# Retention plus gated MLP on one core: loads held behind TensorE products, and a new order of all engines' work

## The chip, the core and the metric

The kernel runs on one core of a Trainium2 chip. The metric is the device time of one execution in microseconds, the median over several runs. A profiled execution gives a trace of every engine; its span goes from the first to the last instruction, and a little lies around it.

## The reference

Inputs are q, k, v of shape 4 x 8 x 768 x 64 (batch, heads, tokens, head size) and the weights of a gated layer of width 512. First a retention layer runs over the tokens:

```
state = gamma[h] * state + outer(k[t], v[t])
y[t]  = q[t] @ state / sqrt(64)
```

Its heads side by side are x (4 x 768 x 512). Then:

```
gate = sigmoid(sum over 5 taps of conv_w[i] * x[t - 4 + i])
out  = (gate * (x @ w_val)) @ w_out
```

## The kernel before, in words

**Tiles.** Tokens are cut into 6 chunks of 128. One tile of q, k, v and k again by token, for one batch and one chunk, is "att" number g (0 to 23, four batches for each chunk); it is 1 MB, or 768 KB in chunk 0, where the fourth part is made on chip. Four att buffers rotate (LB = 4).

**Attention.** The four tiles of chunk 0 have steps of their own: turn (L338, a transpose), wide_scores (L251), wide_mask (L289, VectorE), wide_y (L307) and wide_state (L326). For every later g, TensorE runs block(g) (function block): outputs from the masked scores (y_scores, L348), the state update of this tile and of the next one (L228), outputs from the state (y_state, L348) and the scores of tile g + 1 (L207). Before it VectorE has to mask the scores (mask, L216), ScalarE has to copy the state (snap, L238), and GpSimd has to weigh the values of tile g + 1 by the decay (decay, L198). VectorE then takes the result out of PSUM (evac, L401).

**Weights.** The eight weight tiles (512 KB each) come as 64-bit floats and are converted by some five VectorE steps with help from ScalarE and GpSimd (cv_bits L466 and L472, cv_top L478, cv_exp L484, cv_rest L488, cv_round L512, cv_low L516) into a high and a low part.

**Gated layer.** For each chunk n and each quarter m of the width: four convolution taps on VectorE (tap, L529) and one on ScalarE (L527), a sigmoid (L536), twelve TensorE products val(n, m, 0 to 11) (L543), the gating product on VectorE (gated, L552), a rounded and a rest part (L559 ScalarE, L563 GpSimd). Then, for each batch b, twelve products outp(n, b, 0 to 11) (L571), a copy (store, L581) and the DMA out (send, L585). A val or outp product is one 128x128 by 128x512 matmul; there are 576 of them (some of the last ones cut in halves). Two PSUM buffers ("mm") hold their sums, so a third tile waits until the first has been taken out.

**What sets the order.** The code first collects 1,217 steps (function `at`), each with its engine and what it reads and writes, sorted by a due time. The tuple TURNS then lists the numbers of these steps in the order in which they are issued; `plan` only asserts that the list is allowed. Every engine and every DMA queue executes its own steps in the order of TURNS, and waits in place when the next one isn't ready. All loads and stores go through SyncE's queue (SP), apart from the small fall table. A load waits only until its buffer is free. A -1 in TURNS is a fill: one 128x512 matmul on zeros (function fill, L313), which computes nothing. There are 17.

Of the kernel before, what the change touches and what calls it, by code (L numbers as in the profile page):

```python
# [16 lines left out]
P = 128  # L17
# [8 lines left out]
GV = 6  # L26
TINY = 2.0 ** -15 * (1.0 + 1.0 / 8.0 - 2.0 ** -23)
# [20 lines left out]
def plan(steps, turns, fill):  # L48

    steps = sorted(steps, key=lambda s: s.due)  # L50
# [36 lines left out]
    return [steps[i] if i >= 0 else fill for i in turns]  # L87
# [3 lines left out]
def tile_retention_gated_mlp(  # L91
# [32 lines left out]
    nc = tc.nc  # L124
# [37 lines left out]
    steps = []  # L162
# [11 lines left out]

    def load(g, part=slice(0, 4)):
        b, c = chunks[g]
        i = b * NCH + c
        if g not in tiles:
            tiles[g] = loads.tile([P, 4, 2, 2, P], F32, name="att")
        src = att[i, :, part]  # L180
        if g in PIECES_OF:
            size = P * 4 * P
            src = att[i].rearrange("p a x j n -> (p a x j n)")[part.start * size:part.stop * size].rearrange(
                "(p a x j n) -> p a x j n", p=P, x=2, j=2, n=P
            )
        nc.sync.dma_start(out=tiles[g][:, part], in_=src)  # L186
# [125 lines left out]
    def fill():  # L312
        nc.tensor.matmul(  # L313
            z_ps[:, 0].rearrange("p b j e -> p (b j e)"),
            lhsT=warm.broadcast_to([P, P]), rhs=warm.broadcast_to([P, 512]),
            start=not begun, stop=True, skip_group_check=True,
        )
# [103 lines left out]
    def load_w(n):  # L421
# [7 lines left out]
        nc.sync.dma_start(out=st, in_=src)  # L429
# [108 lines left out]
    def val(n, m, i):  # L538
# [4 lines left out]
        nc.tensor.matmul(  # L543
# [4 lines left out]
        )  # L548
# [16 lines left out]
    def outp(n, b, i, cs):  # L565
        if i == 0:
# [4 lines left out]
        nc.tensor.matmul(  # L571
            ops[n, b, cs.start][:, 0:cs.stop - cs.start],
            lhsT=gg[:, b * P:(b + 1) * P],
            rhs=w[:, ct, cs],
            start=(i == 0), stop=(i == 3 * NPAIR - 1),
        )
# [11 lines left out]
    def first_sigmoid():  # L588
# [345 lines left out]
    with tc.manual_schedule():  # L934
        for step in plan(steps, TURNS, Step(0.0, "PE", 0.2345, [], [], fill, ())):
            step.fn(*step.args)
# [104 lines left out]
```

## Time and profile before

| | |
|---|---|
| median of 3 runs | 212.74 us (212.64 to 212.78) |
| profiled execution | 212.19 us, span 210.5 us |
| TensorE busy in the span | 200.7 us (95%) |
| VectorE, ScalarE, GpSimd busy | 135.7, 110.1, 105.6 us |
| DMA | 35.18 MB, mean 167 GB/s |

The busy times are means over stages that differ: until about 47 us the engines share the start, afterwards TensorE works without a gap that matters. So the table says little about the start, which has to be read by stretches, by the chain of work that ended last, and by timelines of single engines.

### The profile page before, as it was taken

How to read it: one execution, taken by the hardware profiler on the slowest of the kernel's cores; microseconds unless marked ns; L12 is line 12 of the kernel's file. 1: busy time of each engine (PE TensorE's matmuls, PEld its weight loads, DVE VectorE, ACT ScalarE, POOL GpSimd, SP SyncE). 2: the span in 40 equal slices, each digit the busy share in tenths (PEclk: the TensorE clock that was granted, in tenths of full speed). 3: DMA queues.
4: the chain of work that ended last, by engine and by line, in shares of the span. 5: the costliest groups of instructions: out<-in, count | busy, mean ns of one | idle time of the engine just before them, and what ended most of it. 6: DMA issues, size and time to landing. Idle time of an engine off the chain costs nothing.

```text
span 210.5 us, 7499 instructions
## 1 busy us (share of the span) xinstructions
PE 200.7 (95%) x3322; PEld 159.9 (76%) x3325; DVE 135.7 (64%) x209; ACT 110.1 (52%) x228; POOL 105.6 (50%) x98
## 2 busy tenths in 40 slices
PE   8699699999899999999999999999999999999993
PEld 3578477778678888888888878787878777877783
DVE  1987999999999952469528791625867357671000
ACT  2478988598736925382534643516460654523321
POOL 1477699899964238830266731422920456132200
PEclk9999889999999999999999999999999999999998
DMA  6999998576602984519725270011110111111122
GB/s 214 375 417 379 402 404 307 198 291 218 223 14 69 360 350 178 206 52 348 277 79 156 101 246 23 35 55 53 53 50 0 50 53 50 50 50 50 51 102 100
DMA packets 8402, 35.18 MB, mean 167 GB/s; under 512 B 937, under 2 KB 1193, under 8 KB 5810
## 3 DMA queue, kind: packets, MB, share of 16 engines
q1 hardware_dynamic: 8352, 34.66, 44.5%
q8 instruction: 26, 0.43, 0.9%
q10 hardware_dynamic: 18, 0.04, 0.1%
q14 instruction: 6, 0.05, 0.1%
HBM read 28.41 MB, written 6.29 MB: 165 GB/s over the span
## 4 chain that ended last, share of the span: by engine, by line
PE 79%; DVE 9%; DMA 4%; ACT 2%; issue 2%; SPq 1%; DVEq 0%; ACTq 0%
PE mm L571 32%; PE mm L543 28%; PE sy L348 9%; DMA att<-in_att_dram 4%; DVE acc L529 3%; PE sy L207 3%; PE z_ps L228 3%; PE z_ps L326 1%; PE sy L251 1%; DVE top L478 1%; SPq L186 1%; DVE acc L484 1%; PE mm L307 1%; DVE acc L472 1%; DVE rest L488 1%
## 5 line engine op out<-in xcount | busy, mean ns | idle before, releaser
L529 DVE SCALAR_TENSOR_TENSOR acc<-x,cw_sb,acc 128x512 f32<-128x512 f32 x96 | 69.4, 751 | 7.2 <-ACT acc L527 6.4
L563 POOL TENSOR_TENSOR gvl<-gate,gvh 128x512 fp32r<-128x512 f32 x24 | 31.0, 1293 | 51.9 <-ACT gvh L559 50.8
L581 ACT COPY o_sb<-mm 128x512 f32<-128x512 f32 (+1 forms) x25 | 14.2, 569 | 47.2 <-PE mm L571 47.1
L571 PE MATMUL mm<-woh,gvh 128*128 128x512 f32 (+1 forms) x100 | 38.9, 393 | 0.0
L571 PE MATMUL mm<-wol,gvh 128*128 128x512 f32 (+1 forms) x100 | 38.5, 387 | 0.0
L571 PE MATMUL mm<-woh,gvl 128*128 128x512 f32 (+1 forms) x100 | 38.4, 386 | 0.0
L552 DVE TENSOR_TENSOR gate<-mm,gate 128x512 f32<-128x512 f32 x24 | 16.6, 690 | 33.0 <-PE mm L543 30.4
L414 POOL TENSOR_TENSOR xl<-x,xh 128x512 fp32r<-128x512 f32 x24 | 30.6, 1289 | 11.0 <-ACT xh L410 11.0
L543 PE MATMUL mm<-xh,wvh 128*128 128x512 f32 x96 | 32.3, 413 | 1.3 <-ACT xh L410 1.3
L198 POOL TENSOR_TENSOR att<-att,first_sb 128x512 f32<-128x512 f32 x24 | 25.0, 1047 | 15.7 <-DMA att<-in_att_dram 13.0
L543 PE MATMUL mm<-xh,wvl 128*128 128x512 f32 x96 | 30.4, 399 | 0.7 <-issue 0.7
L543 PE MATMUL mm<-xl,wvh 128*128 128x512 f32 x96 | 30.3, 397 | 0.5 <-POOL xl L414 0.5
L536 ACT ACTIVATE gate<-acc 128x512 f32<-128x512 f32 x24 | 14.4, 598 | 16.9 <-DVE acc L529 11.1
L571 PEld LDWEIGHTS mm<-woh,gvh 128*128 128x128 f32 x100 | 18.7, 188 | 5.4 <-ACT o_sb L581 1.3
L543 PEld LDWEIGHTS mm<-xh,wvl 128*128 128x128 f32 x96 | 18.0, 188 | 5.5 <-issue 1.0
L543 PEld LDWEIGHTS mm<-xh,wvh 128*128 128x128 f32 x96 | 17.4, 188 | 6.0 <-ACT xh L410 1.4
L571 PEld LDWEIGHTS mm<-woh,gvl 128*128 128x128 f32 x100 | 18.8, 188 | 4.1
L543 PEld LDWEIGHTS mm<-xl,wvh 128*128 128x128 f32 x96 | 17.8, 188 | 5.1 <-POOL xl L414 1.2
L571 PEld LDWEIGHTS mm<-wol,gvh 128*128 128x128 f32 x100 | 18.8, 188 | 3.7
L401 DVE TENSOR_TENSOR x<-sy,dec 128x512 f32<-128x512 f32 x20 | 13.8, 688 | 10.2 <-PE sy L207 9.4
L559 ACT CAST gvh<-gate 128x512 fp32r<-128x512 f32 x24 | 14.9, 619 | 6.9 <-DVE gate L552 4.4
L410 ACT CAST xh<-x 128x512 fp32r<-128x512 f32 x24 | 14.6, 622 | 6.2 <-DVE x L401 3.1
(65 smaller groups left out, 266.1 us busy)
## 6 DMA issues: line engine op xcount, KB each, us to landing
att<-in_att_dram SPq DMA_DIRECT2D x20, 1024.0 KB, 6.1
out_dram<-o_sb SPq DMA_DIRECT2D x23, 256.0 KB, 2.1
wst<-in_w_dram SPq DMA_DIRECT2D x7, 512.0 KB, 7.7
att<-in_att_dram SPq DMA_DIRECT2D x3, 768.0 KB, 8.3
first_sb<-in_first_dram SPq DMA_DIRECT2D x1, 568.0 KB, 3.9
att<-in_att_dram SPq DMA_DIRECT2D x1, 512.0 KB, 5.0
att<-in_att_dram SPq DMA_DIRECT2D x1, 256.0 KB, 6.0
out_dram<-o_sb SPq DMA_DIRECT2D x2, 128.0 KB, 1.8
```

What stands on the lines that cost most here:

```text
L198: nc.gpsimd.tensor_tensor(v, v, vd_sb[:, c, :].unsqueeze(2).broadcast_to([P, 8, HALF]), op=ALU.mult)
L348: return nc.tensor.matmul(sy[cols, h, off:off + HALF], lhsT=lhsT, rhs=rhs, start=start, stop=True, skip_group_check=True,)
L410: nc.scalar.copy(xh[n, ct], xs[n][:, ct, :, HALO:])
L414: nc.gpsimd.tensor_tensor(xl[n, ct], xs[n][:, ct, :, HALO:], xh[n, ct].bitcast(F32), op=ALU.subtract)
L529: nc.vector.scalar_tensor_tensor(acc, x[:, :, k:k + P], cw_sb[:, m, k:k + 1], acc, op0=ALU.mult, op1=ALU.add,)
L536: nc.scalar.activation(gate[n, m], accs.pop((n, m)), AF.Sigmoid)
L543: nc.tensor.matmul(vps[n, m], lhsT=w[:, m, ct * P:(ct + 1) * P], rhs=xx[n, ct].rearrange("p b t -> p (b t)"), start=(i == 0), stop=(i == 3 ...
L552: nc.vector.tensor_tensor(gv, vps.pop((n, m)), gv, op=ALU.mult)
L559: nc.scalar.copy(gvs[n, m][0], gate[n, m])
L563: nc.gpsimd.tensor_tensor(gvl, gate.pop((n, m)), gvh.bitcast(F32), op=ALU.subtract)
L571: nc.tensor.matmul(ops[n, b, cs.start][:, 0:cs.stop - cs.start], lhsT=gg[:, b * P:(b + 1) * P], rhs=w[:, ct, cs], start=(i == 0), stop=(i ...
L581: nc.scalar.copy(o_sb[:, 0:step], ops.pop((n, b, cs.start))[:, 0:step])
```

## The change

It has three parts.

**Loads held.** Every val and outp product is appended to a list. Each load (att tiles and weight tiles, not the stores) that is issued when at least four products are in the list gets one more wait: on the fourth-last product issued so far. With the new order that holds for 19 loads: att 8 to 23 and weight tiles 5, 4 and 7.

**Fills of two sizes.** A -1 is a fill of 512 columns, a -2 one of 128. The new list has five -1 and four -2. The six fills with which TensorE began are gone; it begins with one fill of 128, first_pos and the two outer steps.

**A new TURNS.** The same 1,217 steps in another order, on all engines and queues. From block(22) on TensorE's order is the old one. Before, among other things:

- loads begin: weight 0, att 0 (q and k), weight 1, att 1, att 3, att 0 (v), att 2, weights 3 and 2, att 4, 5, 6, weight 6, att 7, 8, 9, weights 5 and 4. Before: weight 0, att 0 (q, k), att 0 (v), weight 2, att 1, att 2, weight 3, att 3, weight 1, att 4, 5, weight 4, att 6, weight 6, att 7, weight 7, att 8, weight 5;
- the table counts what lies ahead of some blocks in either list:

| ahead of | VectorE steps up to its mask, before / after | products, before / after |
|---|---|---|
| block(4) | 30 / 30 | 1 / 2 |
| block(6) | 48 / 48 | 24 / 24 |
| block(8) | 65 / 62 | 42 / 44 |
| block(9) | 70 / 70 | 48 / 52 |
| block(10) | 79 / 77 | 69 / 69 |
| block(12) | 94 / 95 | 85 / 89 |
| block(13) | 100 / 99 | 108 / 120 |
| block(15) | not counted | 139 / 168 |
| block(17) | not counted | 163 / 240 |

- tiles of the gated layer come in another order (in chunk 0 the stores go out as b = 3, 1, 0, 2);
- stores and loads are mixed differently on SP. Att 22 is now the last load: it stands behind outp(2, 0, 7), so it waits for outp(2, 0, 4). Of its tile, block(21) needs the decayed values. TensorE's list between the two is: outp(2,0) 5 to 9, val(3,2) 9 to 11, block(20), outp(2,1) 0 to 8, five more outp, block(21).

The diff, with TURNS cut:

```diff
@@ -24,6 +24,7 @@
 GV = 6
+LAG = 4
-def plan(steps, turns, fill):
+def plan(steps, turns, fills):
...
-    return [steps[i] if i >= 0 else fill for i in turns]
+    return [steps[i] if i >= 0 else fills[-1 - i] for i in turns]
...
+    products = []
+
+    def hold(dma):
+
+        if len(products) >= LAG:
+            tc.add_manual_dep(
+                dma.ins, products[-LAG].ins.name,
+                mybir.DependencyInfo(mybir.DependencyClass.Sync, mybir.DependencyReason.DATA),
+                reason="loads keep clear of the fetch of the program",
+            )
+
     def load(g, part=slice(0, 4)):
...
-        nc.sync.dma_start(out=tiles[g][:, part], in_=src)
+        hold(nc.sync.dma_start(out=tiles[g][:, part], in_=src))
...
-    def fill():
+    def fill(size):
         nc.tensor.matmul(
-            z_ps[:, 0].rearrange("p b j e -> p (b j e)"),
-            lhsT=warm.broadcast_to([P, P]), rhs=warm.broadcast_to([P, 512]),
+            z_ps[:, 0].rearrange("p b j e -> p (b j e)")[:, 0:size],
+            lhsT=warm.broadcast_to([P, P]), rhs=warm.broadcast_to([P, size]),
...
-        nc.sync.dma_start(out=st, in_=src)
+        hold(nc.sync.dma_start(out=st, in_=src))
...
-        nc.tensor.matmul(
+        products.append(nc.tensor.matmul(
             vps[n, m],
...
-        nc.tensor.matmul(
+        products.append(nc.tensor.matmul(
             ops[n, b, cs.start][:, 0:cs.stop - cs.start],
...
     TURNS = (
-        12, -1, 6, 4, 5, 0, 13, 11, -1, 1, 14, -1, 16, -1, 15, -1, 19, -1, 18, 8, 17, 7, 10, -1, 20, -1, 28,
+        12, 6, 5, 1, 2, 13, 11, 4, 0, 20, 15, 17, 14, 19, -2, 28, 8, 29, 7, 18, 10, 46, 59, 60, 21, 53,
+        16, 70, 22, -2, -1, -2, -1, -1, 32, 81, 61, 62, 63, 64, 23, 65, 24, 66, 33, 9, 26, 25, 94, 35,
...
     with tc.manual_schedule():
-        for step in plan(steps, TURNS, Step(0.0, "PE", 0.2345, [], [], fill, ())):
+        for step in plan(steps, TURNS, [Step(0.0, "PE", 0.2345, [], [], fill, (n,)) for n in (512, 128)]):
             step.fn(*step.args)
```

## Rows read from the trace of the kernel before

**Rows 1.** The page: span, and busy us (share) with count by engine.
```profile
span 210.5 us, 7499 instructions
PE 200.7 (95%) x3322; PEld 159.9 (76%) x3325; DVE 135.7 (64%) x209; ACT 110.1 (52%) x228; POOL 105.6 (50%) x98
```

**Rows 2.** Stretches: length, busy us (instructions) by engine, granted TensorE clock, DMA share, GB/s.
```profile
20.00:25.00 5.00, 3.12 (x82) 2.31 (x83) 4.57 (x8) 4.79 (x11) 3.37 (x5) 0.97 1.02 407
25.00:30.00 5.00, 4.87 (x133) 4.24 (x134) 4.91 (x8) 4.02 (x9) 3.90 (x4) 0.69 1.00 408
45.00:50.00 5.00, 4.92 (x141) 4.00 (x140) 5.00 (x9) 5.00 (x14) 5.00 (x5) 1.00 0.63 220
150.00:155.00 5.00, 5.00 (x23) 3.82 (x21) 4.12 (x7) 1.31 (x3) 2.76 (x3) 1.00 0.15 56
```

**Rows 3.** The chain that ended last: start us, us, what.
```profile
24.93 0.76 DVE acc L529
...
46.45 0.61 DVE u L216
...
47.11 0.69 PE sy L348 x32
...
49.20 1.60 PE mm L543 x6
50.81 0.69 PE sy L348 x32
...
54.78 0.71 issue
...
67.18 0.62 PE sy L348 x32
...
103.76 1.64 PE mm L571 x7
...
125.41 0.62 PE sy L348 x32
...
127.28 0.67 PE mm L543 x2
...
194.00 12.78 PE mm L571 x65
```

**Rows 4.** VectorE between the masks of blocks 4 and 9: timeline, then the stretch.
```profile
23.39 0.68 DVE L216 TENSOR_TENSOR u<-sy,tri_sb 128x512 f32<-128x512 f32 x1
...
49.47 0.69 DVE L216 TENSOR_TENSOR u<-sy,tri_sb 128x512 f32<-128x512 f32 x1
...
23.39:49.47 26.08, 25.41 (x41) 0.93 0.78 297
```

**Rows 5.** TensorE's timeline at the start: start us, us, line, what, count [idle before <-releaser].
```profile
0.84 2.72 PE L313 MATMUL z_ps<-const-float32-0.0 128*128 128x512 bf16 x6 [0.84 <-PEq L1028]
...
10.94 1.16 PE L251 MATMUL sy<-att 64*128 64x128 f32 x16 [0.25 <-DMA att<-in_att_dram]
12.03 0.66 PE L338 MATMUL mm<-eye_sb,att 128*128 128x128 f32 x4
12.95 0.63 PE L338 MATMUL mm<-eye_sb,att 128*128 128x128 f32 x4 [0.26 <-DMA att<-in_att_dram]
...
20.42 1.05 PE L307 MATMUL mm<-gvl,att 128*64 128x128 f32 x16
21.85 0.46 PE L228 MATMUL z_ps<-att 64*64 64x64 f32 x16 [0.39 <-POOL att L198]
22.14 0.65 PE L207 MATMUL sy<-att 64*64 64x64 f32 x32
...
25.12 1.14 PE L348 MATMUL sy<-u,att 64*64 64x64 f32 x32 [0.31 <-issue]
...
28.75 1.34 PE L543 MATMUL mm<-xh,wvh 128*128 128x512 f32 x4
```

**Rows 6.** Att loads: SP's waits for TensorE, landing times; the decay step on GpSimd.
```profile
SPq L186 <- PE sy L348: 36.9, 11, 7.3
...
DMA to landing us min/median/max: 4.8/6.1/9.6
...
L198 POOL TENSOR_TENSOR att<-att,first_sb x24: 1042/1046/1056, 9.6 to 126.9; 128x512 f32<-128x512 f32 x24
```

More of the change, by code (lines that the diff above doesn't have):

```diff
@@ L547, in val @@
             start=(i == 0), stop=(i == 3 * NPAIR - 1),
-        )
+        ))
     def gated(n, m):
@@ L575, in outp @@
             start=(i == 0), stop=(i == 3 * NPAIR - 1),
-        )
+        ))
     def store(n, b, cs=slice(0, DM)):
```

127 rows, old and new, of the table TURNS are left out of this document.

## The prediction

> **What bounds the kernel now.** First the page: TensorE is busy 95% of the span [rows 1], so the question is where its other time lies. The stretches answer that: from 45 us on TensorE fills nearly every stretch, at a granted clock of 1.00; between 20 and 30 us it is busy for 3.12 of 5 us, and then works at a mean granted clock of 0.69, while VectorE is busy 4.57 to 5.00 of 5 us throughout [rows 2]. The chain names the bound of each part: from 24.93 us it runs nearly without a break over VectorE, up to the mask of block(8) at 46.45; from 47.11 to 206.78 us it is TensorE's own work, apart from one gap of 0.71 us at 54.78 in which TensorE waits for nothing that the profile shows [rows 3]. So whatever is gained has to come out of the first 50 us or out of that gap; the TensorE work from 67.18 to 206.78 us [rows 3] is fixed, since the change moves steps and removes none but fills.
>
> **Before VectorE's chain: the mask of block(4).** The old list reached this mask at 23.39 us, when VectorE came to it; the scores that it reads had been written at about 22.79 (22.14 and 0.65) [rows 4, 5]. Both lists put 30 VectorE steps up to it. What changes is the loads. In the old queue 568 + 512 + 256 + 512 + 768 + 768 = 3384 KB were queued up to att 2, and TensorE got it at 12.95; 768 KB earlier att 1 at 10.94 [rows 5], so 768 KB take 2.0 us. In the new queue the values of att 0 end at the same 3384 KB, so about 12.95 us, and att 2 768 KB later, so 14.96, 0.2 us before it is asked for. By 12.95 TensorE has done the first two score tiles and three transposes. From 12.95 on the old list needed until about 21.33 (20.42 and some 0.9) for two transposes, two score tiles, four state steps and three wide_y [rows 5]; that is 8.38 us. The new list has one wide_y more (1.02) and one transpose fewer (0.6) to do: 8.8 us, so 21.75. The old one then went on at 21.85 after 0.39 us of waiting for GpSimd, and its scores came 0.94 us later; the new one gives 22.7. I take 22.7 for the mask of block(4): 0.7 us earlier. Bounds: 22.2 if a load comes half a microsecond earlier, 24.4 if the clock is half (below).
>
> **VectorE from block(4) to block(12).** Between the masks of blocks 4 and 9 VectorE ran 40 steps in 26.08 us and was busy for 25.41 of them [rows 4], so 0.652 us a step with all its waits. In the new list the same two masks are 40 steps apart too, but four more products stand ahead of block(9) (52 against 48). VectorE therefore stays the bound for longer, down to block(12), where 95 steps stand ahead against 94, with 89 products against 85. The mask of block(12) then starts 95 - 30 = 65 steps behind that of block(4), 65 x 0.652 = 42.4 us, at 65.1; block(12) follows 0.66 us after its mask starts (46.45 to 47.11 [rows 3]): 65.75. TensorE by itself would not be later: block(9) at 22.7 + 26.08 + 0.66 = 49.4, then three blocks of 2.09 (47.11 to 49.20) and 0.2 for the slower product behind each (0.67 for two at 127.28 where two others take 0.47), and 37 products of 0.233 (1.64 for seven) [rows 3] give 64.9. That leaves 0.85 us for a gap such as the one at 54.78, which is gone or hidden here.
>
> **The sum.** The old block(12) started at 67.18 us [rows 3]. The new one starts 1.43 us earlier, and 4 products (0.93 us) fewer are left behind it. Behind block(12) VectorE is no bound: the mask of block(13) is four steps further (2.6 us), while TensorE has 31 products and a block ahead (9.5 us). So TensorE ends 2.36 us earlier. The profiled execution took 212.19 us; less 2.36 that is 209.83. The median of the runs shown lies 0.55 above it, so I predict 210.4 us.
>
> **What I cost at nothing.** Twelve 512-column fills fewer and four small ones more: the old ones ran while TensorE waited for loads or VectorE, so that their time becomes waiting. The held loads: most already waited for the block that frees their buffer (SP stood 36.9 us in 11 waits for TensorE [rows 6]), and their fourth-last product lies ahead of that block or within a dozen products behind it, ten microseconds or more ahead of the block that needs the tile. Att 20 and 22 are held longer; only att 22 is close, see (d). Behind a held load SP queues stores, whose four buffers reach four tiles back. GpSimd's decay of att 8 now stands ahead of that of att 7, which block(6) needs: att 8 is released some 4 us behind the start of block(4) and landed in 6.1 us at the median [rows 6], so both decays (1.05 us each) end near the moment when block(6) asks for them; VectorE's next step that reads block(6) comes seven steps later and covers a microsecond.
>
> **Half clock.** TensorE began with six fills, 2.72 us long [rows 5]. At 25.12 us, after the thin stretch, block(4) took 3.63 us (to 28.75) where block(8) took 2.09 [rows 2, 3, 5]. Those six fills go. [...] If only the first score tile runs at half speed, its 1.1 us more end before att 1 lands, about 10.3 us, and cost nothing: my sum. If the run behind 12.95 us is slow for as long as block(4) was, 1.7 us are lost in it.
>
> **Rivals.** (a) *Half clock in the run of chunk 0*: the mask of block(4) at 24.4, the gain 0.66 us, 212.1. For it: fewer fills, and TensorE still waits for loads. Against it: the fills that stay, and transposes that are drawn forward into the wait. (b) *VectorE denser*: 0.61 us a step, as between 25 and 30 us (8 steps, 4.91 us busy [rows 2]); then TensorE's own 64.9 shrinks with block(9) to 63.2 and decides, and the gain is 67.18 - 63.2 + 0.93 = 4.9 at most, 207.9; a gap of 0.71 makes it 208.6. (c) *The change doesn't do what it says*: the held loads don't change what TensorE waits for, steps on VectorE take 0.69 us because conversions wait for ScalarE and GpSimd in line, and 65 x 0.038 = 2.5 us are given back: 212.9. (d) *Slower: att 22 comes late.* It waits for outp(2,0,4). Between that and the state update in block(21) lie 22 products (5.13 us), block(20) (127.28 - 125.41 = 1.87, and 0.2) and 0.62 us of block(21): 7.8 us [rows 3]. In them the load must be issued (0.3), land and be decayed (1.05): it may take 6.4 us. Landings took 4.8 to 9.6 us, 6.1 at the median [rows 6]. TensorE has no slack there, so each microsecond beyond is lost in full: at 9.6 us 3.2 are lost, 213.6, slower than before by 0.8. It is slower than before from 8.8 us on. Against it: the long landings belong to the start, when 400 GB/s were moved [rows 2]; at 150 us the DMA engines are 15% busy.
>
> **How the numbers follow.** My forecast has a chance of 0.54, (a) 0.12, (b) 0.10, (c) 0.08, (d) 0.16. A measurement tells 0.2%, 0.43 us, from no change. The forecast and (b) are faster by more, and half of (a): 0.70. Half of (a) and half of (c) are the same: 0.10. The other half of (c) and (d) are slower: 0.20. The range takes in (b) with its gap, (a), (c) and most of (d): 208.6 to 213.2. The forecast's own range is 209.2 to 211.8, by 0.2 us on the mask of block(4) and 0.02 us on a step either way.
>
> **What would show it.** Right: the chain goes over VectorE until about 65 us and then over TensorE alone; the mask of block(4) starts near 22.7, that of block(9) near 48.8, and block(12) near 65.8; no gap at TensorE behind that. Wrong: a clock of 0.5 behind 12 us; the chain leaving VectorE at block(8) as before; GpSimd waiting for a load ahead of a decay and TensorE for that decay, above all before block(21); gaps at TensorE in which it waits for nothing that shows, each of them a loss once TensorE is the bound.

## The result and the profile after

The changed kernel took **210.12 us** (median of 4 runs, 209.52 to 211.15), the kernel before 212.76 (212.64 to 213.04) beside it: a ratio of 0.9884, with a 95% interval of 0.9853 to 0.9915. Run again beside the experiments it gave 0.9916 (0.9883 to 0.9948). The profiled execution took 210.03 us, against the 209.83 of the sum. Its page, to set beside [rows 1]; the last line is the share of the chain that ended last:

```profile
span 208.3 us, 7483 instructions
PE 199.1 (96%) x3317; PEld 160.4 (77%) x3317; DVE 136.2 (65%) x209; ACT 110.3 (53%) x228; POOL 105.8 (51%) x98
...
PE 82%; DMA 7%; POOL 4%; ACT 3%; issue 1%; DVE 0%; ACTq 0%; POOLq 0%; SPq 0%
```

VectorE has next to no share in the chain (0%, one piece of 0.70 us at 43.24), where it was to carry it until 65 us. The stretches, to set beside [rows 2]:

```profile
20.00:25.00 5.00, 4.12 (x126) 3.09 (x120) 4.90 (x9) 3.53 (x9) 3.18 (x4) 1.00 0.99 339
25.00:30.00 5.00, 4.31 (x98) 3.56 (x93) 4.76 (x8) 4.36 (x11) 4.78 (x5) 1.00 0.92 359
45.00:50.00 5.00, 4.93 (x147) 3.51 (x149) 5.00 (x9) 4.97 (x12) 5.00 (x5) 1.00 0.64 206
```

From 20 to 25 us TensorE is busy for 4.12 us instead of 3.12, and from 25 to 30 its clock stays at 1.00 instead of 0.69. The masks that the forecast named, from VectorE's timeline (those of blocks 4, 9 and 12; [rows 4] has the first two of before):

```profile
22.77 0.69 DVE L228 TENSOR_TENSOR u<-sy,tri_sb 128x512 f32<-128x512 f32 x1
...
48.78 0.68 DVE L228 TENSOR_TENSOR u<-sy,tri_sb 128x512 f32<-128x512 f32 x1
...
64.60 0.68 DVE L228 TENSOR_TENSOR u<-sy,tri_sb 128x512 f32<-128x512 f32 x1
```

They were forecast for 22.7, 48.8 and 65.1. **All three times come out within half a microsecond, and yet the chain goes elsewhere** (to set beside [rows 3]):

```profile
14.14 12.79 DMA att<-in_att_dram x2
26.93 0.22 issue
27.15 1.04 POOL att L210
28.20 1.30 POOL wvl L528
29.50 4.32 POOL xl L426 x4
...
34.43 2.07 POOL att L210 x2
36.49 0.04 issue
36.54 0.46 PE z_ps L240 x16
...
52.49 4.16 PE mm L555 x17
...
65.75 0.62 PE sy L360 x32
...
191.85 12.76 PE mm L583 x65
```

It comes over a load and GpSimd's row of rests and decays to 36.5 us, and then over TensorE, but for 43.24 to 50.82 us, where short pieces of ScalarE carry it behind the one of VectorE. So TensorE ends at 204.61 us, 2.17 earlier than the 206.78 of before.

**Where the 2.17 us come from.** Read from TensorE's timelines, block(4) starts at 23.59 instead of 25.12, 1.53 us earlier; only 0.62 of that is the mask (22.77 against 23.39). In the old list a product that waits 1.30 us for ScalarE's rounding, then a fill and a wait of 0.31, stood between the scores and block(4); the new list has a wait of 0.22 there. TensorE's timeline, of before (its block(4) is in [rows 5]) and of after:

```profile
24.08 0.49 PE L543 MATMUL mm<-xh,wvh 128*128 128x512 f32 x1 [1.30 <-ACT xh L410]
```
```profile
22.92 0.73 PE L555 MATMUL mm<-xh,wvh 128*128 128x512 f32 x2 [0.22 <-ACT xh L422]
23.59 0.69 PE L360 MATMUL sy<-u,att 64*64 64x64 f32 x32
```

This is one execution of each. In the other profiled ones of the experiments block(4) started between 23.70 and 24.84 us with the new order, and at 25.68 and 26.16 with the old one where it got no more products, so the 1.53 is known to about a microsecond. From block(4) to block(12) both kernels take the same time within 0.1 us. These are the stretches between the two, first of before, then of after:

```profile
25.12:67.11 41.99, 40.66 (x1109) 32.08 (x1112) 40.85 (x64) 30.51 (x66) 35.74 (x31) 0.96 0.60 219
```
```profile
23.59:65.68 42.09, 40.24 (x1115) 32.02 (x1114) 41.51 (x66) 31.73 (x68) 36.80 (x31) 1.00 0.73 270
```

In those 42.09 us the new list gets three products more done (0.7 us). TensorE is even busy for 0.42 us less, since block(4) no longer runs at half clock (granted 0.50 from 25 to 28 us before, 1.00 after). Then 0.74 us are saved behind block(12), because four products fewer are left (1.43 + 0.74 = 2.17).

All of TensorE's waits behind 20 us, from the view of waits (what waited <- for what: us in total, times, longest):

```profile
PE z_ps L240 <- POOL att L210: 1.2, 3, 0.7
PE z_ps L240 <- ACT snap L250: 0.6, 2, 0.3
PE mm L555 <- ACT xh L422: 0.2, 1, 0.2
PE sy L360 <- issue: 0.2, 1, 0.2
PE sy L360 <- PE sy L360: 0.2, 1, 0.2
```

There is no wait before block(21): att 22 was not late, so rival (d) did not come.

### The profile page after: what moved, and what is told of

Its sections match the earlier page's. It is cut to its first block, busy times and chain, and to the rows that moved or that the text cites. A ratio compares the mean times of both kernels' runs of the same rounds, so it can differ in the third digit from the quotient of the medians.

```text
span 208.3 us, 7483 instructions
## 1 busy us (share of the span) xinstructions
PE 199.1 (96%) x3317; PEld 160.4 (77%) x3317; DVE 136.2 (65%) x209; ACT 110.3 (53%) x228; POOL 105.8 (51%) x98
## 4 chain that ended last, share of the span: by engine, by line
PE 82%; DMA 7%; POOL 4%; ACT 3%; issue 1%; DVE 0%; ACTq 0%; POOLq 0%; SPq 0%
PE mm L583 32%; PE mm L555 29%; PE sy L360 9%; DMA att<-in_att_dram 6%; PE sy L219 4%; PE z_ps L240 3%; POOL xl L426 2%; POOL att L210 1%; PE sy L263 1%; DMA wst<-in_fall_dram 1%; PE mm L350 1%; PE z_ps L325 1%; ACT xh L422 1%; POOL wvl L528 1%; ACT snap L250 1%
## 5 line engine op out<-in xcount | busy, mean ns | idle before, releaser
L541 DVE SCALAR_TENSOR_TENSOR acc<-x,cw_sb,acc 128x512 f32<-128x512 f32 x96 | 70.4, 752 | 5.5 <-ACT acc L539 4.3
L583 PE MATMUL mm<-woh,gvh 128*128 128x512 f32 (+1 forms) x100 | 38.3, 389 | 0.0
L555 PE MATMUL mm<-xh,wvh 128*128 128x512 f32 x96 | 30.7, 408 | 0.3 <-ACT xh L422 0.2
L555 PE MATMUL mm<-xh,wvl 128*128 128x512 f32 x96 | 29.0, 400 | 0.0
L250 ACT COPY snap<-z_ps 128x256 f32<-128x256 f32 x40 | 14.0, 374 | 9.1 <-PE z_ps L240 6.5
L539 ACT ACTIVATE acc<-x,cw_sb 128x512 f32<-128x512 f32 x24 | 16.5, 695 | 3.8 <-DVE rest L500 3.6
```

What stands on the lines that cost most here:

```text
L250: nc.scalar.copy(sn, z_ps[:, :, b])
L539: nc.scalar.mul(acc, x[:, :, 0:P], cw_sb[:, m, 0:1])
L541: nc.vector.scalar_tensor_tensor(acc, x[:, :, k:k + P], cw_sb[:, m, k:k + 1], acc, op0=ALU.mult, op1=ALU.add,)
L555: products.append(nc.tensor.matmul(vps[n, m], lhsT=w[:, m, ct * P:(ct + 1) * P], rhs=xx[n, ct].rearrange("p b t -> p (b t)"), start=(i == ...
L583: products.append(nc.tensor.matmul(ops[n, b, cs.start][:, 0:cs.stop - cs.start], lhsT=gg[:, b * P:(b + 1) * P], rhs=w[:, ct, cs], start=(i ...
```

## The experiments

### 1. The waits of the loads: the change without them, and the old order with them

`c_after` is the changed kernel once more. `e_nohold` takes the added waits away, `e_before_hold` puts them alone into the kernel before.

```diff
 e_nohold, against the changed kernel
-        hold(nc.sync.dma_start(out=tiles[g][:, part], in_=src))
+        nc.sync.dma_start(out=tiles[g][:, part], in_=src)
...
-        hold(nc.sync.dma_start(out=st, in_=src))
+        nc.sync.dma_start(out=st, in_=src)
```

> The changed kernel once more, beside which the others of this call are read. Both theories: 0.988 to 0.991 of the kernel before.

> The changed kernel without the added waits of the loads; order and fills as changed. Theory 'order' (the time comes from the new order, the waits only follow the blocks that free the buffers): within 0.4 us of the changed kernel, about 0.988 of before, and the same start of block(4), 23.6 us. Theory 'hold' (loads that keep clear of the fetch of the program save gaps at TensorE): some 0.7 us or more slower than the changed kernel, about 0.992 or worse, with gaps of 0.3 to 0.7 us before products or blocks, for which the profile shows no releaser.

> The kernel before with nothing but the waits of the loads added. Theory 'order': within 0.4 us of the kernel before, or slower, since the old list wasn't made for later loads. Theory 'hold': the gap of 0.71 us at 54.78 is gone and the kernel is 0.7 us faster, about 0.9965.

`c_after` 0.9916 (0.9883 to 0.9948); `e_nohold` **1.0042** (1.0017 to 1.0066); `e_before_hold` 0.9985 (0.9968 to 1.0002). So the waits that I costed at nothing are worth about 1.3% of the time, 2.5 us (medians of 213.48 and 211.03), in the new order, and next to nothing in the old one. The new order without them is slower than the kernel before. TensorE's timeline of `e_nohold` shows the place, inside block(11):

```profile
62.82 0.65 PE L360 MATMUL sy<-att,snap 64*64 64x64 f32 x32
63.29 0.41 PE L219 MATMUL sy<-att 64*64 64x64 f32 x16
65.40 0.46 PE L219 MATMUL sy<-att 64*64 64x64 f32 x16 [1.70 <-issue]
```

TensorE stops halfway through a group of 32 equal matmuls, for 1.70 us, with its operands there: by the counts below I take it to have run out of program. Just ahead of it a load (att 14) moves at 352 GB/s. Stretches of `e_nohold` and, for the same place, of the changed kernel:

```profile
60.00:62.00 2.00, 2.00 (x17) 1.36 (x19) 1.98 (x4) 2.00 (x6) 2.00 (x3) 1.00 0.89 352
62.00:64.00 2.00, 1.70 (x112) 1.60 (x109) 1.89 (x3) 1.05 (x4) 1.38 (x2) 1.00 0.37 147
```
```profile
58.00:60.00 2.00, 2.00 (x54) 1.72 (x46) 2.00 (x4) 1.97 (x5) 1.81 (x2) 1.00 0.83 344
60.00:62.00 2.00, 2.00 (x65) 1.51 (x66) 1.97 (x4) 1.81 (x5) 1.49 (x2) 1.00 0.33 53
```

The trace also records transfers of instructions: the queue "q8 instruction" on the page, 26 packets and 0.43 MB, 16 KB each. I take them for TensorE's program, since its gaps follow them and a count of its instructions fits them. Counted in the traces (weight loads, matmuls and the recorded waits of its queue), TensorE stops in the gaps of the table in part 2 after 705, 1473, 2241, 2753 or 4545 instructions, and each of these is 193 more than a multiple of 256. (In two traces with three matmul records missing it is 2238 instead of 2241.) So I take a packet to hold 256 instructions, an estimate from these counts. In the 350 fetches of the fourteen profiled executions for which this place can be counted, TensorE never begins the instruction behind it earlier than 1.2 us after its packet has landed.

The packet that belongs here started when TensorE had begun 1252 matmuls in the changed kernel (59.90 us), and 1347 in `e_nohold` (63.19 us). 95 matmuls later, that is, and behind the load: the program that TensorE had at hand ends 1368 matmuls in, so 116 were left in the one kernel and 21 in the other. In both the packet starts when the load ahead of it is over (328 and 238 GB/s in the microsecond before, 0 in the one behind).

The gap is 1.70 of the 2.06 us by which `e_nohold` takes longer from block(4) to block(12) (44.15 us against 42.09). TensorE ends 3.0 us later than in the changed kernel, by these two profiles; the other parts (0.57 us by block(4), 0.37 behind block(12)) have no such gap, and their cause is not shown.

### 2. Is it one load? Only att 14 held, and all but att 14

```diff
 g_only14, against the changed kernel (the weight loads are sent without hold)
-        hold(nc.sync.dma_start(out=tiles[g][:, part], in_=src))
+        dma = nc.sync.dma_start(out=tiles[g][:, part], in_=src)
+        if g == 14:
+            hold(dma)
 g_not14
+        if g != 14:
+            hold(dma)
```

> The changed kernel with one load alone held back, the fifteenth att load (att 14), and every other load sent as soon as its buffer is free. The changed kernel with no load held ran at 1.004 of the kernel before and lost 1.70 us in one gap of block(11). Theory (one load of 256 KB stands in front of one fetch of TensorE's instructions): the gap of 1.7 us is gone and the ratio is 0.990 to 0.994. Rival (many loads cost a little each): the gap is gone at most in part, and the ratio stays at 0.999 to 1.003.

> The mirror: the changed kernel with every load held except att 14, which goes as soon as its buffer is free. Theory of the one load: a gap of 1 us or more ended by issue is in block(10) or block(11) and the ratio is 0.996 to 1.003. Rival: within 0.5 us of the changed kernel, 0.987 to 0.992, with no such gap.

(Att 14 is 1024 KB, not 256.) `g_only14` 0.9939 (0.9912 to 0.9967), between the two; `g_not14` 0.9900 (0.9868 to 0.9932), like the changed kernel. The first result half fits the theory of the one load, the second refutes it: att 14 was issued 2.8 us ahead of block(11) there, nearly as early as in `e_nohold` (3.2) and not as late as in the changed kernel (0.8). The gap in block(11) is gone in both, and in `g_only14` there is a new one, four blocks earlier:

```profile
42.44 0.21 PE L362 MATMUL sy<-u,att 64*64 64x64 f32 x1 [1.41 <-issue]
```

Ahead of it loads run that are held in the changed kernel. One-microsecond stretches of `g_only14`, and one of them for the changed kernel, where the loads pause (373 GB/s before it, 225 and 418 behind it):

```profile
38.00:39.00 1.00, 1.00 (x6) 0.83 (x5) 1.00 (x3) 1.00 (x4) 0.70 (x1) 1.00 1.06 410
39.00:40.00 1.00, 1.00 (x6) 0.79 (x5) 1.00 (x3) 0.73 (x2) 1.00 (x2) 1.00 0.94 348
40.00:41.00 1.00, 1.00 (x32) 0.55 (x31) 1.00 (x3) 0.68 (x3) 1.00 (x2) 1.00 0.60 233
41.00:42.00 1.00, 0.04 (x3) 0.00 (x0) 0.96 (x2) 0.97 (x2) 1.00 (x1) 1.00 0.83 328
```
```profile
39.00:40.00 1.00, 1.00 (x6) 0.82 (x5) 1.00 (x3) 0.82 (x3) 1.00 (x2) 1.00 0.63 94
```

The fetch started after 699 matmuls (40.01 us) here, after 695 in the changed kernel (39.15): four products later in the work, and TensorE stands still from 41.03. So it is not a matter of one load: in `e_nohold` the late fetch stood behind one, in `g_only14` behind another. Nor does the rate ahead of a fetch decide alone: the one of 59.90 in the changed kernel had 434 and 328 GB/s in the two microseconds before it, and no gap behind it. What goes with the gap is how much of the program TensorE has left when the fetch starts (116 matmuls against 21 above), and how fast it gets through it: a block is 128 matmuls in 2.1 us, in which it gets through only nine products (0.233 us each).

All gaps of TensorE of 0.2 us or more that begin behind 26 us and are ended by "issue", in all kernels of this study, agree with this (us; the last column is the end of the gap less the end of the fetch):

```
kernel          fetch starts   takes   gap              behind the fetch
before             53.19       0.99    54.78 to 55.49       1.31
e_before_hold      25.45       0.97    26.82 to 27.70       1.28
e_before_hold      53.90       0.99    55.51 to 56.31       1.42
b_clock            25.52       0.97    26.83 to 27.81       1.32
b_clock            53.94       0.96    54.38 to 56.12       1.22
b_clock           101.45       1.01   103.38 to 103.93      1.47
h_notap_before     53.66       0.99    55.33 to 55.88       1.23
e_warm             52.42       1.04    54.39 to 54.67       1.21
b_clock_notap      54.20       1.00    54.79 to 56.48       1.28
e_nohold           63.19       0.95    63.70 to 65.40       1.26
g_only14           40.01       1.00    41.03 to 42.44       1.43
after              39.15       0.97    41.31 to 41.52       1.40
```

In each, TensorE goes on 1.2 to 1.5 us after a fetch has landed. (Gaps of the old order ahead of 26 us, such as 0.31 us at 24.81, don't follow a fetch in this way.) The gap at 54.78 that I called "gone or hidden" is such a one; the old kernel has loads at 401 to 410 GB/s from 51 to 53 us. The waits alone leave it in place in the old order (0.81 us in `e_before_hold`, and another of 0.88 at 26.8).

### 3. Does VectorE set the pace? A convolution tap less in either kernel

```diff
 h_notap_after, h_notap_before
     def tap(n, m, k):
+        if n == 0 and k == 4:
+            return
```

> The changed kernel without the fifth convolution tap of chunk 0 (four VectorE steps, at 0.652 us each 2.6 us of VectorE before mask 4). Theory V (VectorE bounds the changed kernel until block(12)): the mask of block(12) comes up to 2.6 us earlier, and TensorE, which by itself needs until 64.9, ends some 0.8 us earlier: about 0.4% less than the changed kernel. Rival T (from 36 us TensorE, with GpSimd and ScalarE, bounds the changed kernel already): TensorE's end moves by less than 0.4 us.

> The kernel before without the same four steps. Theory V: VectorE bounds this one too until block(12), and TensorE has more to gain: 1.5 to 2.5 us less, ratio 0.988 to 0.993. Rival T: under 0.8 us, ratio above 0.996.

`h_notap_after` 0.9912 (0.9886 to 0.9937), as the changed kernel with it. `h_notap_before` 0.9985 (0.9964 to 1.0006), as the kernel before. **Theory V falls in both.** All four steps lie between the masks of block(4) and block(12), and yet the first and last of these masks in `h_notap_before` stand nearly as far apart as those of the kernel before. First `h_notap_before`, then the last mask of before (its first is in [rows 4]):

```profile
24.23 0.68 DVE L216 TENSOR_TENSOR u<-sy,tri_sb 128x512 f32<-128x512 f32 x1
...
66.17 0.68 DVE L216 TENSOR_TENSOR u<-sy,tri_sb 128x512 f32<-128x512 f32 x1
```
```profile
65.78 0.68 DVE L216 TENSOR_TENSOR u<-sy,tri_sb 128x512 f32<-128x512 f32 x1
```

That is 60 steps in 41.94 us, where the kernel before did 64 in 42.39 (23.39 to 65.78): 0.45 us less for four steps that at 0.652 us would be 2.6. In the changed kernel it is 65 steps in 41.83 us, and 61 in 41.97 without the tap. So the 0.652 us a step are not VectorE's own pace. Where the tap is gone VectorE simply waits longer, and for TensorE; groups of VectorE's instructions in `h_notap_after` from block(4) to block(12) (busy, mean ns, idle before, releaser):

```profile
L413 DVE TENSOR_TENSOR x<-sy,dec 128x512 f32<-128x512 f32 x8 | 5.5, 686 | 2.0 <-PE sy L219 2.0
```

In the changed kernel the same eight waited 0.1 us.

### 4. What did the half clock cost?

`e_warm` puts six fills of 512 columns ahead of the changed kernel's work. `b_clock` puts five into the wait of the old kernel at 22.8 us, ahead of the slow block(4); `b_clock_notap` leaves out the tap as well.

```diff
 e_warm
     TURNS = (
-        12, 6, 5, 1, 2, 13, ...
+        -1, -1, -1, -1, -1, -1, 12, 6, 5, 1, 2, 13, ...
 b_clock, against the kernel before
         if i == 0:
             vps[n, m] = ps_m.tile([P, 512], F32, name="mm")
+            if n == 0 and m == 0:
+                for _ in range(5):
+                    nc.tensor.matmul(
+                        vps[n, m], lhsT=warm.broadcast_to([P, P]), rhs=warm.broadcast_to([P, 512]),
+                        start=True, stop=True, skip_group_check=True,
+                    )
```

> The changed kernel with six fills of 512 columns put ahead of TensorE's work, as the kernel before had them. The first score tile then takes 1.1 us instead of 2.1. By the prediction this time is hidden behind the load of att 1: no change, within 0.3 us of the changed kernel. If the half clock at the start does cost something, it is faster by up to 0.9 us.

> The kernel before with five more 512-column products on zeros, put into the 1.3 us in which TensorE waits at 22.8 us, so that block(4) should run at full clock (2.1 instead of 3.63 us). Theory C (the half clock of block(4) is about 1.5 us of what the change gains): block(8) starts 1 us or more earlier than before, ratio 0.991 to 0.996. Rival (VectorE covers it in the old order): under 0.4 us, ratio 0.998 to 1.001.

> The same, and the four VectorE steps of the fifth tap of chunk 0 left out. Theory of a tie (in the old order VectorE and TensorE are both close to the bound, so that relieving one alone gives little): this run gains 1.3 us or more, ratio 0.989 to 0.994, while either edit alone gives under 0.5 us. Rival (GpSimd's row of rests is the bound until 38 us): under 0.6 us, ratio above 0.997.

`e_warm` 0.9942 (0.9921 to 0.9962): no gain. It could not settle much, since the fills did not raise the speed of what follows. The first score tile took 2.08 us with them and without them, where the next one of the changed kernel took 1.16. First `e_warm`, then the changed kernel:

```profile
6.79 2.08 PE L263 MATMUL sy<-att 64*128 64x128 f32 x16
```
```profile
6.69 2.08 PE L263 MATMUL sy<-att 64*128 64x128 f32 x16
...
10.79 1.16 PE L263 MATMUL sy<-att 64*128 64x128 f32 x16
```

The view of stretches gives a granted clock of 1.00 from 6 to 9 us in both, but in the changed kernel's trace the clock is recorded only from 10.48 us on, so what made this tile slow is open.

`b_clock` did what it was meant to: a granted clock of 1.00 from 25 to 28 us, where the old kernel had 0.50. The time went **up**, to 1.0067 (1.0031 to 1.0103), and with the tap gone to 1.0103 (1.0067 to 1.0139). Both theories are wrong. TensorE's timeline of `b_clock` says why:

```profile
23.77 1.25 PE L543 MATMUL mm<-const-float32-0.0 128*128 128x512 bf16 x5 [0.50 <-ACT x L344]
24.91 0.50 PE L549 MATMUL mm<-xh,wvh 128*128 128x512 f32 x1
...
25.79 0.69 PE L348 MATMUL sy<-u,att 64*64 64x64 f32 x32
26.30 0.53 PE L228 MATMUL z_ps<-att 64*64 64x64 f32 x23
27.81 0.38 PE L228 MATMUL z_ps<-att 64*64 64x64 f32 x9 [0.97 <-issue]
...
56.12 0.63 PE L549 MATMUL mm<-xh,wvh 128*128 128x512 f32 x2 [1.74 <-issue]
```

Block(4) starts at a clock of 1.00 (0.69 us for 32 matmuls, 1.14 before) and then stands still for 0.97 us behind the fetch of 25.52. The slow clock had only hidden that wait: in the old kernel TensorE came to the same place, 705 instructions in, at 27.10 us, 1.3 us after its packet had landed, with nothing to spare. `e_before_hold` shows the same from another side, since its block(4) happened to run at a clock of 1.00 and stood still for 0.88 us there. The gap at 54.8 has grown from 0.71 to 1.74 as well. The five fills are five more matmuls in the program ahead of it, each with its weight load (the six of `e_warm` make 3323 of either on its page, where the changed kernel has 3317), so that a piece of 16 KB ends five products earlier in the work: TensorE runs out behind two products after block(9), where it had seven before, and after the same 2241 instructions. Five products are 1.17 us, and the gap is 1.03 larger. **A fill in a wait is not free**: it takes its place in the program, too. `e_warm`, with six more, has a gap of 0.28 us at 54.39 that the changed kernel lacks. No run shows a gain in time from a wait that was filled.

### 5. GpSimd: two decays in the other order, and two left out

```diff
 s_swap, in TURNS, lines cut short (197 is the decay of att 8, 157 that of att 7)
-        211, 143, 158, 124, 161, 193, 212, 213, 44, 215, 176, 192, 197, 222,
-        216, 191, 159, 160, 223, 157, 194,
+        211, 143, 158, 124, 161, 193, 212, 213, 44, 215, 176, 192, 157, 222,
+        216, 191, 159, 160, 223, 197, 194,
 n_nodecay
     def decay(g):
+        if g in (6, 8):
+            return
```

> The changed kernel with GpSimd's decays of att 8 and att 7 in the other order, so that the one which block(6) needs comes first. Theory: TensorE's gap of 0.17 us in block(6) goes, and nothing else: the ratio is that of the changed kernel (0.988 to 0.992) or at most 0.3 us better. Rival (decay 8 is late then for block(7)): a new gap there.

> The changed kernel with GpSimd's decays of att 6 and att 8 left out (two steps of 1.05 us ahead of the one on which TensorE waits at 36.5 us). Theory G (GpSimd sets the pace of the changed kernel from 27 to 36.5 us): block(6) and all behind it come 0.5 us or more earlier. Rival (TensorE's own work, with many short waits, sets it): under 0.3 us; the ratio stays within 0.988 to 0.992.

`s_swap` 0.9894 (0.9857 to 0.9930), 210.53 us: the 0.17 us are gone and nothing else is, no new gap at block(7). `n_nodecay` 0.9915 (0.9878 to 0.9951): from block(4) to block(6) 11.53 us, against 11.85 in the changed kernel and 11.29 in its second run. So theory G, by which block(6) had to come 0.5 us or more earlier, falls too, although the chain of the changed kernel ran over GpSimd for those nine microseconds. In the chain of `c_after`, the same program, VectorE has a quarter of the stretch from 22 to 38 us:

```profile
by line: DMA att<-in_att_dram 33.9%; DVE acc L541 25.3%; DVE x L413 7.5%; DVE gate L564 7.4%; DVE u L228 7.4%; DVE rest L514 4.3%; DVE acc L484 4.3%; issue 4.2%; POOL rest L507 3.9%; DVE acc L496 3.8%; DVE rest L500 3.7%; DVE top L490 3.7%;
```

So in a stretch where the engines are as close as here the chain named one of them in one execution and another in the next. No version beat the changed kernel by more than the intervals.

## Why the prediction was right, and where it was not

The time (210.4 us against 210.12) and the sign were right, the closeness in part by luck: the same kernel's median was 211.03 when it ran again, and two errors inside the sum cancelled. The steps fare less well.

- **The mask of block(4) at 22.7**: 22.77, and much by the way the forecast named: TensorE went on to the state update ahead of these scores at 21.77 (forecast 21.75), though it had come there 0.34 us earlier and waited for GpSimd's decay. TensorE's own gain at block(4), 1.53 us, is larger than the mask's 0.62, and the forecast had no term for it: in the old list a product that waited for ScalarE's rounding stood there, which the new list places better.
- **VectorE as the bound down to block(12)**: this step failed. Its mask came at 64.60 instead of 65.1, 65 steps in 41.83 us, and block(12) 1.15 us behind it instead of 0.66. The two errors cancel, and block(12) stands in the chain at 65.75, as forecast. The longer wait behind the mask says that TensorE, not the mask, came last there; it was so in the old kernel too (mask of block(9) at 49.47, block(9) at 50.81 [rows 3, 4]), while the 0.66 was read from block(8) alone. Four VectorE steps fewer change nothing in either kernel (experiment 3), nor do two GpSimd steps fewer in the changed one (5). The estimate of TensorE's own time stood in the prediction, 64.9, and I used it only as a check. A run of VectorE pieces in the chain and a busy share of 97% were taken for a bound; what was missing is whether TensorE would have waited less if VectorE had been faster. That relieving TensorE alone would have given nothing either, as in a tie, no run shows: where `b_clock` cured its slow block, a fetch gap took the place.
- **Four products fewer behind block(12), 0.93 us**: 0.74. This is the whole difference between the 2.17 us and the 2.36 of the sum, since block(12) came 1.43 us earlier as forecast.
- **The held loads costed at nothing** ("most already waited for the block that frees their buffer"): this step failed too. In the new order they are worth 2.5 us, about the whole gain (experiment 1). I priced them by the buffers alone, and missed the fetch of TensorE's program, which in experiment 1 started when the load ahead of it was over (at 59.90 us with the waits, at 63.19 without), although the last sentence of the text ("gaps at TensorE in which it waits for nothing that shows, each of them a loss once TensorE is the bound") and the reason written beside the wait pointed to it. Without them the result would have been 1.0042 times the time before, and the forecast wrong in sign. That there is no gap behind block(12) is right for the kernel as it is; without the waits the gap of 1.70 us lies just ahead of block(12).
- **The half clock** (rival a): the first score tile took 2.08 us (1.16 in the kernel before), and the run behind 12.95 us was at full clock (granted 1.00 from 12 to 20 us), as the sum had it. That the fills set the speed of this tile was my estimate: `e_warm`, with six of them, took 2.08 us as well. That the tile cost nothing is not shown: it lies in the chain of the changed kernel (TensorE from 3.56 to 14.08 us), while in `c_after` TensorE waited 0.19 us for a load behind the next tile, until 11.99. My 1.5 us of slow block(4) in the old kernel were not for sale by themselves: where it was cured, a fetch wait of 0.97 us stood in its place (experiment 4).
- **Rival (b)**, a denser VectorE, came at 0.644 us a step instead of 0.61, and then not by VectorE's doing. **(c)** did not come: a step took 0.644 us and not 0.69, and the held loads do change what TensorE waits for. **(d)** did not come: no wait before block(21).

What stays open: how much of the 2.17 us is due to the places in the work at which the pieces of the program end. The new list has eight fills fewer, which moves them as the five of `b_clock` did. In the old order TensorE runs out near 54.8 us, 2241 instructions in, with the loads held or not; in the changed kernel it gets past the same count at 55.09 us, 1.94 us after its packet has landed, without a gap. No run took fills away from the old list alone.

## What to carry to other kernels

A gap that ends with "issue", often in the middle of equal matmuls, was in all twelve cases behind 26 us a fetch of the program that came late. Count the engine's instructions up to the gap and look at what the DMA engines moved in the two microseconds before the fetch; then delay the loads that are not needed yet, or move the place where the piece ends out of a block of short matmuls. The first helped here in one order and did nothing in the other; the second no run tried. A chain that runs over one engine is only a hint of a bound, since another execution of the same kernel can run over another engine. Before a sum is built on an engine's steps per microsecond, work out the time of the next engine as well, and where both come out within a microsecond don't count on a gain from relieving one of them. And a cure for one wait that is stacked on others (a slow clock on a late fetch) should be priced by the next one in the stack.

## What was not expected of the hardware

As I read the records, TensorE's program comes in pieces of 16 KB (queue q8: 26 packets, 0.43 MB), by the counts 256 instructions each. A piece took 0.88 to 1.82 us in the profiled executions of the two kernels, and TensorE got to its first instruction never earlier than 1.2 us after it had landed (350 fetches). In the twelve gaps of the table it stood still for 0.21 to 1.74 us and went on 1.2 to 1.5 us after a piece had landed. TensorE gets through the 128 matmuls of a block in 2.1 us, and with as many weight loads they make 256 instructions, a whole piece. In `b_clock` a wait was filled with products on zeros: the granted clock was 1.00 instead of 0.50 from 25 to 28 us, and the kernel took 0.7% longer.
